# Reading the moving operands of the split products with the words of their two halves in turn

## The chip, the cores and the metric

The kernel runs on one core of one Trainium2 chip. The metric is the device time of one execution, in microseconds, as the median of three runs. The core has five engines that run side by side and wait for one another through semaphores: TensorE (PE, with its weight loads shown as PEld), VectorE (DVE), ScalarE (ACT), GpSimd (POOL, here an issuer of transfers) and SyncE (SP, also an issuer of transfers).

## The reference, cut to what matters

Eight batches of linear attention (8 heads, 576 tokens, 64 wide) feed a gated feed-forward layer over 4608 tokens.

```python
q_s = softmax(q over its last axis);  k_s = softmax(k over the sequence)
kv  = einsum('bhsd,bhse->bhde', k_s, v)
x   = einsum('bhsd,bhde->bhse', q_s, kv)   # -> x: 4608 tokens x 512
gate = sigmoid(x @ w_gate)                 # 512 x 1536
val  = x @ w_val                           # 512 x 1536
out  = (gate * val) @ w_out                # 1536 x 512
```

The three weights come as 64-bit floats and are narrowed on the chip; everything else is in 32-bit floats.

## The kernel before

Tokens go through in nine windows of 512 (`NW`). Window 0 is done while the weights are still being narrowed. For windows 1 to 8 the inner dimension of 1536 is walked in six steps, and one step is `g1` (gate and value for 256 inner columns) followed by `g2` of the step before (the product with `w_out`, added into four accumulators in PSUM). The side work of the next window (softmax of `q` and `k`, the `kv` products, `x` itself in `x_mm`) is laid between them by hand, in `side_a`, `side_b` and `fill`. The order on every engine is the order in which the code is written; nothing reorders it later.

**Split products.** A 32-bit value is written as a high part, which is the value rounded to the type `float32r`, and a low part, the difference. A product is then three matmuls: high times high, high times low, low times high. ScalarE makes the high part (a copy into `float32r`), VectorE the low part (a subtraction). The pairs are `c_hl` (pieces of `x` for `g1`), `wo_hl` and `wo_t` (pieces of `w_out`, the moving operand of `g2`), `x_hl` (window 0's `x`, from inner column block 6 on), and the two `ring` tiles of `qT_split` (the moving operand of `x_mm`). They lie in SBUF as contiguous words, and the matmul reads them as contiguous words. The stationary operands (`a_w`, `s_sb`, `h`, `h_parts`, `kv_sb`) are split too, by other lines.

**Sizes.** One call of `g1` is 7 products of 12 matmuls of 128x128 by 256 columns (L860). One call of `g2` is 25 matmuls (L958): 23 of 512 columns and 2 of 256. There are 48 steps, so 4032 matmuls at L860 and 1200 at L958. In window 0, `g1_0` (L777) and `g2_0` (L826) use plain 32-bit operands for the first blocks, where one matmul becomes two instructions on TensorE, and split operands after that: 144 matmuls at L777 and 84 at L826, of 512 columns. `x_mm` (L659) has 12 products of 512 columns in each window from 1 on, cut in two where a window spans two batches.

**Start.** Until about 26 us there is little for TensorE to do. The kernel fills the gaps with matmuls whose results nobody reads: 11 at first (`warm`, L1179, 32-bit, 128 columns), then two groups between the transposes of `k`. The first group is 4 of 512 `float32r` columns (`warm_whole`, L1194) and 5 in which the 512 columns are one and the same word (`warm_one`, L1198: a step of zero). The second is 5 pairs that use 64 rows each (`warm_rows`, L1187) and 2 more of `warm_whole`. All of them read `kv_sb`, which holds zeros then.

Of the kernel before, what the change touches and what calls it, by code (L numbers as in the profile page):

```python
# [8 lines left out]
F32 = mybir.dt.float32  # L9
# [8 lines left out]
P = 128  # L18
# [3 lines left out]
T = 512  # L22
# [29 lines left out]
def attn_moe(ctx: ExitStack, tc: tile.TileContext, qf, qn, qT, k, kT, v, wg, wv, wo, out):  # L52
# [57 lines left out]
    def flat(ap):  # L110
        return ap.rearrange("p a b -> p (a b)")

# [114 lines left out]
    def wo_hi(j):  # L227
        wo_out[j] = t = whpool.tile([P, 2, DM], F32R, name="wo_hl")
        nc.scalar.copy(out=t[:, 0], in_=wo_t[j // 2][:, j % 2])

    def wo_lo(j):
        t = wo_out[j]
        nc.vector.tensor_tensor(
            out=t[:, 1], in0=wo_t[j // 2][:, j % 2], in1=t[:, 0].bitcast(F32), op=ALU.subtract
        )
# [30 lines left out]
    def wo_split(w, p):  # L266
        for i, t in enumerate(wo_hl[w, p]):
            j = 2 * p + i
            if j in wo_stage:
                x = wo_stage.pop(j)  # L270
                nc.scalar.copy(out=t[:, 0], in_=x)
                nc.vector.tensor_tensor(
                    out=t[:, 1], in0=x, in1=t[:, 0].bitcast(F32), op=ALU.subtract
                )
# [356 lines left out]
    def qT_split(w, hp):  # L631
        t = qT_sb.pop((w, hp))
        hi, lo = (ring.tile([P, T], F32R, name="ring") for _ in range(2))
        nc.scalar.copy(out=hi, in_=t)
        nc.vector.tensor_tensor(out=lo, in0=t, in1=hi.bitcast(F32), op=ALU.subtract)
        qT_hl[w, hp] = (hi, lo)
# [12 lines left out]
    def x_mm(w, hp):  # L649
        qh, ql = qT_hl.pop((w, hp))  # L650
        if w > 1 and hp < 3:
            ps = ps_gv.tile([P, T], F32, name="gv")
        else:
            ps = ps_at.tile([P, T], F32, name="at")
        x_ps[w, hp] = ps
        parts = x_parts(w)
        for lh, rh in ((0, qh), (0, ql), (1, qh)):
            for b, f, t in parts:
                nc.tensor.matmul(  # L659
                    ps[:, f:t], lhsT=kv_sb[:, b % 2, lh, hp], rhs=rh[:, f:t],  # L660
                    start=(lh == 0 and rh is qh and f == 0), stop=(lh == 1 and t == T),
                    skip_group_check=True,
                )
# [30 lines left out]
    def x_split_hi(i):  # L694
        sl = slice(2 * i, 2 * i + 2)
        nc.scalar.copy(out=x_hl[0][:, sl], in_=x_0[:, sl])

    def x_split_lo(i):
        sl = slice(2 * i, 2 * i + 2)
        nc.vector.tensor_tensor(  # L700
            out=x_hl[1][:, sl], in0=x_0[:, sl], in1=x_hl[0][:, sl].bitcast(F32), op=ALU.subtract
        )
# [25 lines left out]
    def c_split_hi(i):  # L728
# [8 lines left out]
        nc.scalar.copy(out=c_hl[i][:, 0], in_=src)  # L737

    def c_split_lo(i):
        hi, lo = (c_hl[i][:, x] for x in range(2))  # L740
        nc.vector.tensor_tensor(
            out=lo, in0=c_src.pop(i), in1=hi.bitcast(F32), op=ALU.subtract
        )
# [16 lines left out]
    def g1_0(j):  # L760
        ps = [ps_gv.tile([P, T], F32, name="gv") for _ in range(2)]
        for n in range(2):
            w = w_f32(j, n)
            for kt in range(NK):
# [3 lines left out]
                else:  # L768
# [5 lines left out]
                    xh, xl = (t[:, kt] for t in x_hl)  # L774
# [41 lines left out]
    def g2_0(j):  # L816
        if j == 0:
            acc_new(0)
        if in_parts(j):
            (h_hi, h_lo), (o_hi, o_lo) = ([t[:, i] for i in range(2)] for t in (h_parts[j], wo_out[j]))  # L820
            pairs = [(h_hi, o_hi), (h_hi, o_lo), (h_lo, o_hi)]
        else:
            pairs = [(h_0[j], wo_t[j // 2][:, j % 2])]
# [26 lines left out]
    def g1(w, p, s_next=None):  # L850
# [4 lines left out]
        def prod(ps, ws, i, first, last):  # L855
            for n in range(2):
                wh, wl = ws(n)
                for kt in range(2):
                    for lh, x in ((wh, 0), (wh, 1), (wl, 0)):
                        nc.tensor.matmul(  # L860
                            ps[:, n], lhsT=lh(kt), rhs=c_hl[i][:, x, kt],
# [78 lines left out]
    def g2(w, at):  # L940
# [6 lines left out]
        for i in range(2):  # L947
            for m in range(NT):
# [7 lines left out]
                for lh, rh, e, halves in order:  # L956
                    es = slice(e * DM // halves, (e + 1) * DM // halves)
                    nc.tensor.matmul(  # L958
                        acc[w][m][:, es], lhsT=h[lh][:, i, sl], rhs=o[i][:, rh, es],
                        start=(at == 0 and i == 0 and lh == 0 and rh == 0),  # L960
                        stop=(at == NS - 1 and i == 1 and lh == 1 and e == halves - 1),
# [177 lines left out]
    many = kv_sb.rearrange("p b i h e -> p (b i h e)")  # L1139
# [41 lines left out]
    beside = ps_at.tile([P, T], F32, name="at")  # L1181

    def warm_rows(n):
        for i in range(n):
            for a, ps in enumerate((idle, beside)):
                sl = slice(a * D, (a + 1) * D)
                nc.tensor.matmul(  # L1187
                    ps, lhsT=many[sl, 0:P], rhs=many[sl, T:2 * T], start=True, stop=True,
                    skip_group_check=True,
                )  # L1190

    def warm_whole(n):
        for i in range(n):
            nc.tensor.matmul(idle, lhsT=many[:, 0:P], rhs=many[:, T:2 * T], start=True, stop=True)  # L1194

    def warm_one(n):
        for i in range(n):
            nc.tensor.matmul(  # L1198
                idle, lhsT=many[:, 0:P], rhs=many[:, T:T + 1].broadcast_to([P, T]),
                start=True, stop=True,  # L1200
            )

# [3 lines left out]
    for i in range(0, NP, 2):  # L1206
# [9 lines left out]
        if i == 0:  # L1216
            warm_whole(4)
            warm_one(5)
        else:
            warm_rows(5)  # L1220
            warm_whole(2)
# [248 lines left out]
```

## Time and profile before

| | us |
|---|---|
| median of three runs | 917.14 (916.32 to 917.47) |
| the profiled execution: its own time | 917.45 |
| the profiled execution: its span on the core | 915.7 |
| TensorE busy (matmuls) in that span | 906.5 |
| VectorE busy | 627.2 |
| ScalarE busy | 496.5 |
| TensorE from the start of the first step of window 1 to the end, on the chain that ended last | 145 to 910 |

The busy time of TensorE counts a matmul until its result is out, while the next one has begun long before; so the time that a matmul costs is read from the distance between starts, and best from a long unbroken run of them. The durations of single matmuls (277 ns for 256 columns) overlap and can't be added.

### The profile page before, as it was taken

The numbers are of one execution on the slowest core, as the hardware profiler recorded it, in microseconds if no ns is written. First come the engines' busy times: TensorE is split into PE (matmuls) and PEld (weight loads), VectorE is DVE, ScalarE is ACT, GpSimd is POOL, SyncE is SP. The second block draws the span as 40 slices with busy tenths as digits, with TensorE's granted clock in tenths as the row PEclk, the third lists the DMA queues.
The fourth block names the chain that finished last, engine by engine and source line by source line (L and its number), as shares of the span: only waits on it lengthen the run. The fifth ranks groups of instructions, "written<-read, shape, count | busy, mean of one in ns | idle before, by whom it ended". The sixth has DMA issues, their size and how long they took to land.

```text
span 915.7 us, 16619 instructions
## 1 busy us (share of the span) xinstructions
PE 906.5 (99%) x6481; PEld 810.1 (88%) x6481; DVE 627.2 (68%) x1021; ACT 496.5 (54%) x845; POOL 186.1 (20%) x342
## 2 busy tenths in 40 slices
PE   8999999999999999999999999999999999999997
PEld 7445788999999999999999999999999999999996
DVE  7899999878686567657684777567755565553332
ACT  6989995657473546363554456445633443443212
POOL 0112112324121222122212121212211222121210
PEclk9999999999999999999999999999999999999999
DMA  9997567987998989997999699969997799668771
GB/s 336 382 357 241 211 237 265 309 314 269 311 331 270 344 248 357 319 276 207 371 318 284 184 360 339 287 196 339 336 271 225 212 276 335 197 194 252 220 206 50
DMA packets 91839, 252.62 MB, mean 276 GB/s; under 512 B 13872, under 2 KB 14128, under 8 KB 91760
## 3 DMA queue, kind: packets, MB, share of 16 engines
q0 software_dynamic: 45200, 163.08, 56.7%
q1 hardware_dynamic: 46560, 88.48, 31.3%
q8 instruction: 51, 0.84, 0.4%
q14 instruction: 28, 0.23, 0.1%
HBM read 217.97 MB, written 33.54 MB: 275 GB/s over the span
## 4 chain that ended last, share of the span: by engine, by line
PE 87%; DVE 5%; DMA 4%; ACT 1%; issue 1%; SPq 1%; ACTq 0%
PE gv L860 48%; PE acc L958 28%; PE gv L777 3%; PE gv L659 2%; PE acc L826 2%; PE at L496 2%; PE at L659 1%; DMA wo_raw<-wo_in 1%; DMA q_b<-q_m_row 1%; DMA lent<-v_in 1%; DMA q_m_row<-q_m 1%; DMA lent<-qf_in 1%; DVE a_w L357 1%; DVE q_m L567 1%; DVE f_w L180 1%
## 5 line engine op out<-in xcount | busy, mean ns | idle before, releaser
L860 PE MATMUL gv<-c_hl,s_sb 128*128 128x256 f32 x2304 | 278.0, 277 | 0.4 <-DMA s_sb<-s 0.4
L860 PEld LDWEIGHTS gv<-c_hl,s_sb 128*128 128x128 f32 x2304 | 269.2, 188 | 0.7 <-DVE x L812 0.6
L860 PE MATMUL gv<-c_hl,a_w 128*128 128x256 f32 x1728 | 221.1, 277 | 0.1
L860 PEld LDWEIGHTS gv<-c_hl,a_w 128*128 128x128 f32 x1728 | 208.5, 188 | 0.5 <-ACT sg L908 0.2
L373 POOL DMA_DIRECT2D s_sb<-s x164 | 88.3, 539 | 281.9 <-PE gv L860 272.2
L958 PE MATMUL acc<-wo_hl,h 128*128 128x512 f32 x589 | 142.6, 391 | 0.0
L958 PE MATMUL acc<-wo_t,h 128*128 128x512 f32 (+1 forms) x613 | 135.8, 372 | 0.0
L958 PEld LDWEIGHTS acc<-wo_t,h 128*128 128x128 f32 x613 | 114.8, 188 | 23.7
L906 DVE TENSOR_TENSOR sg<-gv,sg 128x512 f32<-128x512 f32 x48 | 33.1, 690 | 146.4 <-PE gv L860 146.4
L958 PEld LDWEIGHTS acc<-wo_hl,h 128*128 128x128 f32 x589 | 107.0, 188 | 20.5
L893 ACT COPY sg<-gv 128x512 f32<-128x512 f32 x48 | 28.0, 584 | 110.3 <-PE gv L860 107.7
L908 ACT COPY sg<-gv 128x512 f32<-128x512 f32 x48 | 28.2, 586 | 96.7 <-PE gv L860 96.7
L911 DVE TENSOR_TENSOR sg<-sg 128x512 f32<-128x512 f32 x48 | 33.2, 691 | 52.5 <-ACT sg L908 52.5
L932 DVE TENSOR_TENSOR h<-sg,h 128x1024 fp32r<-128x1024 f32 x48 | 58.8, 1225 | 1.6
L262 POOL DMA_DIRECT2D wo_hl<-wo x44 | 26.1, 592 | 159.8 <-PE acc L958 159.8
L920 DVE TENSOR_TENSOR sg<-sg 128x512 f32<-128x512 f32 x48 | 33.2, 692 | 36.3 <-ACT sg L914 36.3
L914 ACT ACTIVATE sg<-sg 128x512 f32<-128x512 f32 x48 | 30.3, 632 | 46.1 <-DVE sg L913 46.0
L902 ACT COPY sg<-gv 128x512 f32<-128x512 f32 x48 | 28.2, 587 | 36.3 <-PE gv L860 36.3
L899 ACT COPY sg<-gv 128x512 f32<-128x512 f32 x48 | 28.2, 587 | 35.0 <-PE gv L860 35.0
L262 POOL DMA_DIRECT2D wo_t<-wo x45 | 24.2, 539 | 95.8 <-PE acc L958 95.6
L777 PE MATMUL gv<-x,f_w 128*128 128x512 f32 x96 | 42.0, 592 | 0.0
L777 PEld LDWEIGHTS gv<-x,f_w 128*128 128x128 f32 x96 | 18.2, 190 | 23.0 <-issue 21.8
(188 smaller groups left out, 1209.9 us busy)
## 6 DMA issues: line engine op xcount, KB each, us to landing
s_sb<-s POOLq DMA_DIRECT2D x164, 512.0 KB, 6.5
wo_t<-wo POOLq DMA_DIRECT2D x45, 512.0 KB, 6.6
wo_hl<-wo POOLq DMA_DIRECT2D x44, 512.0 KB, 4.4
s<-s_sb POOLq DMA_DIRECT2D x24, 512.0 KB, 7.5
out<-x SPq DMA_DIRECT2D x35, 256.0 KB, 6.8
ring<-k_in SPq DMA_DIRECT2D x28, 256.0 KB, 9.2
ring<-qn_in SPq DMA_DIRECT2D x28, 256.0 KB, 6.3
q_b<-q_m_row SPq DMA_DIRECT2D x56, 128.0 KB, 9.5
```

The lines of the kernel that those rows point to most:

```text
L262: nc.gpsimd.dma_start(out=t.rearrange("p h e -> p (h e)"), in_=wo_dram[j].bitcast(F32R))
L373: nc.gpsimd.dma_start(out=s_of(i).rearrange("p h n e -> p (h n e)"), in_=s_dram[p][:, i * n:(i + 1) * n].bitcast(F32R),)
L777: nc.tensor.matmul(ps[n], lhsT=a, rhs=x, start=(kt == 0 and i == 0), stop=(kt == NK - 1 and i == len(pairs) - 1),)
L860: nc.tensor.matmul(ps[:, n], lhsT=lh(kt), rhs=c_hl[i][:, x, kt], start=(first and n == 0 and kt == 0 and lh is wh and x == 0), stop=(last ...
L899: nc.scalar.copy(out=sg[:, 2], in_=z)
L902: nc.scalar.copy(out=sg[:, 1], in_=y)
L906: nc.vector.tensor_tensor(out=sg[:, 0], in0=rr, in1=sg[:, 0], op=ALU.add)
L911: nc.vector.tensor_tensor(out=sg[:, 3], in0=sg[:, 3], in1=sg[:, 2], op=ALU.add)
L914: nc.scalar.activation(sg[:, 0:2, 0], sg[:, 0:2, 0], AF.Sigmoid)
L920: tt(out=sg[:, 0:2, 0], in0=sg[:, 0:2, 0], in1=sg[:, 0:2, 1], op=ALU.mult)
L932: nc.vector.tensor_tensor(out=lo, in0=sg[:, :, 0], in1=hi.bitcast(F32), op=ALU.subtract)
L958: nc.tensor.matmul(acc[w][m][:, es], lhsT=h[lh][:, i, sl], rhs=o[i][:, rh, es], start=(at == 0 and i == 0 and lh == 0 and rh == 0), stop=( ...
```

## The change

Three helpers are added. `halves` looks at the last axis of a tile as two halves, each contiguous. `apart` looks at a source as pairs of neighbouring words, the even words first and the odd ones after them: it steps two words at a time. `woven` looks at a tile as words of its first half and its second half in turn.

The splits that make moving operands read their source through `apart` and write through `halves`. So the even words land in the first half of the tile and the odd words in the second. The matmuls read the tile through `woven`, and get the words back in their old order: word 0 of half one, word 0 of half two, word 1 of half one, and so on. The two words of a turn lie 512 bytes apart in `c_hl` (256 columns) and 1024 bytes apart in `wo_hl`, `wo_t`, `x_hl` and `ring` (512 columns). What is computed, the order of the columns in PSUM, the tiles, their addresses and all waits stay. The stationary operands and the plain 32-bit products are read as before. In `g2` a variable called `halves` is renamed `parts`.

```diff
+    def woven(x):
+        return x.rearrange("p (two t) -> p t two", two=2)
+
+    def apart(x):
+        if len(x.shape) == 3:
+            return x.rearrange("p k (t two) -> p k two t", two=2)
+        return x.rearrange("p (t two) -> p two t", two=2)
+
+    def halves(x):
+        if len(x.shape) == 3:
+            return x.rearrange("p k (two t) -> p k two t", two=2)
+        return x.rearrange("p (two t) -> p two t", two=2)
...
     def wo_hi(j):
-        nc.scalar.copy(out=t[:, 0], in_=wo_t[j // 2][:, j % 2])
+        nc.scalar.copy(out=halves(t[:, 0]), in_=apart(wo_t[j // 2][:, j % 2]))
...
     def x_mm(w, hp):
-                    ps[:, f:t], lhsT=kv_sb[:, b % 2, lh, hp], rhs=rh[:, f:t],
+                    ps[:, f:t], lhsT=kv_sb[:, b % 2, lh, hp], rhs=woven(rh)[:, f // 2:t // 2],
...
     def c_split_hi(i):
-        nc.scalar.copy(out=c_hl[i][:, 0], in_=src)
+        nc.scalar.copy(out=halves(c_hl[i][:, 0]), in_=apart(src))
     def c_split_lo(i):
         nc.vector.tensor_tensor(
-            out=lo, in0=c_src.pop(i), in1=hi.bitcast(F32), op=ALU.subtract
+            out=halves(lo), in0=apart(c_src.pop(i)), in1=halves(hi.bitcast(F32)),
+            op=ALU.subtract,
         )
...
     def g1_0(j):
-                    xh, xl = (t[:, kt] for t in x_hl)
+                    xh, xl = (woven(t[:, kt]) for t in x_hl)
...
     def g2_0(j):
+            o_hi, o_lo = woven(o_hi), woven(o_lo)
...
     def g1(w, p, s_next=None):
-                            ps[:, n], lhsT=lh(kt), rhs=c_hl[i][:, x, kt],
+                            ps[:, n], lhsT=lh(kt), rhs=woven(c_hl[i][:, x, kt]),
...
     def g2(w, at):
+                    ts = slice(e * HT // parts, (e + 1) * HT // parts)
-                        acc[w][m][:, es], lhsT=h[lh][:, i, sl], rhs=o[i][:, rh, es],
+                        acc[w][m][:, es], lhsT=h[lh][:, i, sl], rhs=woven(o[i][:, rh])[:, ts],
...
-        if i == 0:
-            warm_whole(4)
-            warm_one(5)
-        else:
-            warm_rows(5)
-            warm_whole(2)
+        warm(8)
```

`wo_lo`, `wo_split`, `qT_split`, `x_split_hi` and `x_split_lo` change in the same way as the splits shown. The functions `warm_rows`, `warm_whole` and `warm_one` go, and each of the two groups at the start becomes `warm(8)`: eight 32-bit matmuls of 128 columns on a tile of ones.

On no engine does an instruction of the work change its place. Only the groups of filling matmuls at the start do. On TensorE, from the first transposes of `k` (L466) to the first `kv` products (L482, into the PSUM tiles `at`), the rows before are these, cut where the transposes come again:

```order
L1179 MATMUL gv<-lent 128x128 x11
L466 MATMUL acc<-ident,lent 128x128 x4
L466 MATMUL gv<-ident,lent 64x128
...
L1194 MATMUL gv<-kv_sb 128x512 x4
L1198 MATMUL gv<-kv_sb 128x512 x5
...
L1187 MATMUL gv<-kv_sb 128x512
L1187 MATMUL at<-kv_sb 128x512
...
L1194 MATMUL gv<-kv_sb 128x512 x2
L482 MATMUL at<-lent 128x128 x10
```

With the change, the same place (the lines are numbered anew: `warm` is L1199, the transposes L481, the `kv` products L497):

```order
L1199 MATMUL gv<-lent 128x128 x11
L481 MATMUL acc<-ident,lent 128x128 x4
L481 MATMUL gv<-ident,lent 64x128
...
L1199 MATMUL gv<-lent 128x128 x8
L481 MATMUL acc<-ident,lent 128x128 x4
...
L1199 MATMUL gv<-lent 128x128 x8
L497 MATMUL at<-lent 128x128 x10
```

The transposes and the `kv` products stand where they stood; nine and twelve filling matmuls between them have become eight and eight of another kind.

## Rows read from the trace of the kernel before

**Rows 1.** The page: engines' busy time; the chain that ended last, by line.

```profile
PE 906.5 (99%) x6481; PEld 810.1 (88%) x6481; DVE 627.2 (68%) x1021; ACT 496.5 (54%) x845; POOL 186.1 (20%) x342
...
PE gv L860 48%; PE acc L958 28%; PE gv L777 3%; PE gv L659 2%; PE acc L826 2%; PE at L496 2%; PE at L659 1%; DMA wo_raw<-wo_in 1%; DMA q_b<-q_m_row 1%; DMA lent<-v_in 1%; DMA q_m_row<-q_m 1%; DMA lent<-qf_in 1%; DVE a_w L357 1%; DVE q_m L567 1%; DVE f_w L180 1%
```

**Rows 2.** Stretches: engines' busy us, last the clock, DMA share, GB/s.

```profile
45.00:50.00 5.00, 5.00 (x13) 2.24 (x12) 5.00 (x8) 5.00 (x7) 0.00 (x0) 1.00 1.03 419
300.00:400.00 100.00, 100.00 (x780) 93.65 (x779) 68.97 (x111) 53.09 (x97) 21.37 (x39) 1.00 1.01 310
```

**Rows 3.** Chain, in order of time: start us, us, what and how many.

```profile
91.46 3.06 PE gv L777 x12
...
136.60 5.60 PE gv L777 x24
142.20 2.74 PE acc L826 x12
...
288.81 9.54 PE gv L860 x84
298.34 5.46 PE acc L958 x25
...
318.81 2.31 PE gv L659 x18
321.12 0.77 PE at L659 x6
```

**Rows 4.** TensorE's start, in order of time: start us, us, group, [idle before].

```profile
7.59 1.18 PE L1194 MATMUL gv<-kv_sb 128*128 128x512 f32 x4
8.61 1.25 PE L1198 MATMUL gv<-kv_sb 128*128 128x512 f32 x5
10.55 0.66 PE L466 MATMUL acc<-ident,lent 128*128 128x128 f32 x4 [0.69 <-ACT lent L409]
...
15.69 2.61 PE L482 MATMUL at<-lent 128*128 128x128 f32 x14 [0.69 <-DMA lent<-v_in]
18.23 3.08 PE L482 MATMUL acc<-lent 128*128 128x128 f32 x20
21.24 1.99 PE L621 MATMUL gv<-ident,lent 128*128 128x128 f32 x16
23.06 3.60 PE L683 MATMUL acc<-q,f_last 128*128 128x512 f32 x8
26.50 13.90 PE L777 MATMUL gv<-x,f_w 128*128 128x512 f32 x32
```

**Rows 5.** The same view, from 7.9 to 8.2 us only.

```profile
7.90 0.86 PE L1194 MATMUL gv<-kv_sb 128*128 128x512 f32 x3
```

**Rows 6.** Groups of TensorE by line and shape: busy us, mean ns of one.

```profile
L777 PE MATMUL gv<-x,f_w 128*128 128x512 f32 x96 | 42.0, 592 | 0.0
...
L1198 PE MATMUL gv<-kv_sb 128*128 128x512 f32 x5 | 1.3, 380 | 0.0
```

**Rows 7.** Groups of VectorE: busy us, mean ns of one, idle before.

```profile
L447 DVE TENSOR_TENSOR ring<-ring,kmax_b 128x512 f32<-128x512 f32 x28 | 29.3, 1095 | 0.0
...
L629 DVE TENSOR_TENSOR ring<-ring,q_b 128x512 f32<-128x512 f32 x28 | 17.4, 683 | 0.0
...
L180 DVE SCALAR_TENSOR_TENSOR f_w<-f_w,w_raw 128x512 int32<-128x512 int32 x10 | 6.5, 683 | 0.0
```

**Rows 8.** Groups of ScalarE: the same columns.

```profile
L737 ACT CAST c_hl<-ring 128x512 fp32r<-128x512 f32 x32 | 19.1, 618 | 0.0
...
L173 ACT ACTIVATE f_w<-w_raw 128x512 f32<-128x512 f32 x10 | 6.4, 692 | 0.0
```

**Rows 9.** Who waited for whom: us in total, times, longest us.

```profile
POOL s_sb L373 <- PE gv L860: 272.2, 159, 11.0
POOL wo_hl L262 <- PE acc L958: 159.8, 40, 11.8
DVE sg L906 <- PE gv L860: 146.4, 42, 7.6
```

**Rows 10.** Transfers: KB each, median us from issue to landing.

```profile
s_sb<-s POOLq DMA_DIRECT2D x164, 512.0 KB, 6.5
wo_t<-wo POOLq DMA_DIRECT2D x45, 512.0 KB, 6.6
```

More of the change, by code (lines that the diff above doesn't have):

```diff
@@ L233, in wo_lo @@
         nc.vector.tensor_tensor(
-            out=t[:, 1], in0=wo_t[j // 2][:, j % 2], in1=t[:, 0].bitcast(F32), op=ALU.subtract
+            out=halves(t[:, 1]), in0=apart(wo_t[j // 2][:, j % 2]),
+            in1=halves(t[:, 0].bitcast(F32)), op=ALU.subtract,
         )
@@ L270, in wo_split @@
                 x = wo_stage.pop(j)
-                nc.scalar.copy(out=t[:, 0], in_=x)
+                nc.scalar.copy(out=halves(t[:, 0]), in_=apart(x))
                 nc.vector.tensor_tensor(
-                    out=t[:, 1], in0=x, in1=t[:, 0].bitcast(F32), op=ALU.subtract
+                    out=halves(t[:, 1]), in0=apart(x), in1=halves(t[:, 0].bitcast(F32)),
+                    op=ALU.subtract,
                 )
@@ L633, in qT_split @@
         hi, lo = (ring.tile([P, T], F32R, name="ring") for _ in range(2))
-        nc.scalar.copy(out=hi, in_=t)
-        nc.vector.tensor_tensor(out=lo, in0=t, in1=hi.bitcast(F32), op=ALU.subtract)
+        nc.scalar.copy(out=halves(hi), in_=apart(t))
+        nc.vector.tensor_tensor(
+            out=halves(lo), in0=apart(t), in1=halves(hi.bitcast(F32)), op=ALU.subtract
+        )
         qT_hl[w, hp] = (hi, lo)
@@ L695, in x_split_hi @@
         sl = slice(2 * i, 2 * i + 2)
-        nc.scalar.copy(out=x_hl[0][:, sl], in_=x_0[:, sl])
+        nc.scalar.copy(out=halves(x_hl[0][:, sl]), in_=apart(x_0[:, sl]))
     def x_split_lo(i):
@@ L700, in x_split_lo @@
         nc.vector.tensor_tensor(
-            out=x_hl[1][:, sl], in0=x_0[:, sl], in1=x_hl[0][:, sl].bitcast(F32), op=ALU.subtract
+            out=halves(x_hl[1][:, sl]), in0=apart(x_0[:, sl]),
+            in1=halves(x_hl[0][:, sl].bitcast(F32)), op=ALU.subtract,
         )
@@ L741, in c_split_lo @@
         nc.vector.tensor_tensor(
-            out=lo, in0=c_src.pop(i), in1=hi.bitcast(F32), op=ALU.subtract
+            out=halves(lo), in0=apart(c_src.pop(i)), in1=halves(hi.bitcast(F32)),
+            op=ALU.subtract,
         )
@@ L955, in g2 @@
                         order[2:] = [(1, 0, e, 2) for e in range(2)]
-                for lh, rh, e, halves in order:
-                    es = slice(e * DM // halves, (e + 1) * DM // halves)
+                for lh, rh, e, parts in order:
+                    es = slice(e * DM // parts, (e + 1) * DM // parts)
+                    ts = slice(e * HT // parts, (e + 1) * HT // parts)
                     nc.tensor.matmul(
-                        acc[w][m][:, es], lhsT=h[lh][:, i, sl], rhs=o[i][:, rh, es],
+                        acc[w][m][:, es], lhsT=h[lh][:, i, sl], rhs=woven(o[i][:, rh])[:, ts],
                         start=(at == 0 and i == 0 and lh == 0 and rh == 0),
-                        stop=(at == NS - 1 and i == 1 and lh == 1 and e == halves - 1),
+                        stop=(at == NS - 1 and i == 1 and lh == 1 and e == parts - 1),
                         skip_group_check=True,
@@ L1138, in attn_moe @@
     ones = lent[4][:, NP * S:NP * S + P]
-    many = kv_sb.rearrange("p b i h e -> p (b i h e)")
     k0 = lent[0][:, 0:NP * 4 * P].rearrange("p (h s) -> p h s", s=4 * P)
@@ L1179, in warm @@
             nc.tensor.matmul(idle[:, 0:P], lhsT=ones, rhs=ones, start=True, stop=True)
[L1181 to L1201, printed above, removed]
     warm(11)
```

## The prediction

> **What bounds the kernel now.** I read the page first: TensorE is busy 906.5 us of a span of 915.7, and the chain that ended last lies on its lines, 48% on L860 and 28% on L958 [rows 1]. Next I read the stretches: from 300 to 400 us TensorE has no gap, at a granted clock of 1.00, while VectorE is busy 69 us and ScalarE 53 of 100 [rows 2]. Who waits agrees: VectorE, and GpSimd's transfers, wait for TensorE's products [rows 9]; hardly anything that TensorE waits for is listed. So after the start the time is the number of columns that stream through TensorE, times the time per column. The order of work matters little; what matters is whether a column can be had for less.
>
> That is read from the chain by pieces. A call of L860 is 84 matmuls of 256 columns in 9.54 us, one of L958 is 12,288 columns in 5.46 us [rows 3]. That is 0.4436 ns and 0.4443 ns per column: the same for short and long matmuls, so it is a price of the column and not of the matmul. [...]
> - 4 matmuls at L1194 read 512 different words each. Three of them start at 7.90 us or after and L1198 starts at 8.61 [rows 4, 5]: 0.237 us each.
> - 5 matmuls at L1198 have the same weights, columns and place, but their 512 words are one word read again and again. They take 1.25 us with the last one's tail of 0.38 [rows 4, 6], so (1.25 - 0.38) / 4 = 0.2175 us each: 0.4248 ns per column.
> [...]
>
> So the array itself takes a column in 0.42 ns. [...]
>
> **The change part by part.** *Reading the halves in turn.* [...] No row shows two places read in turn by TensorE, so the price is bounded from both sides. [...] The worst is the last rival below. I take the one-word row, 0.4248, as the nearest: same instruction, same weights beside it, same type.
>
> Per step: 21,504 columns x 0.4248 = 9.13 us for 9.54, and 12,288 x 0.4248 = 5.22 for 5.46: 0.65 us less. Times 48 steps: 31.0 us. In window 0, the split blocks of L777 take 5.60 us for 12,288 columns and of L826 2.74 us for 6,144 [rows 3]; they would take 5.22 and 2.61. With 6 of the first and 7 of the second: 6 x 0.38 + 7 x 0.13 = 3.2 us. `x_mm` (24 matmuls, 2.31 + 0.77 us, for 6,144 columns [rows 3]) costs 0.50 ns per column because it is cut into short pieces; I count no gain there. Sum: 34.2 us off. [...]
>
> *The splits.* ScalarE now reads its source two words apart. L173 does that today: 692 ns for 512, against 618 for the copy that splits `c_hl` in order [rows 8]. The function differs, so 74 ns is an upper bound. There are 56 splits for `c_hl`, 32 for `q`, 12 for `w_out` and 2 of double size for `x`: 104 x 0.074 = 7.7 us of ScalarE's time in the whole run. It hides behind TensorE, as ScalarE has 47 us in 100 free [rows 2]. It isn't hidden in window 0, where ScalarE and VectorE are busy 5.00 of 5 us [rows 2]: there are 9 + 4 splits and two double ones, 1.3 us. I count 0.5 us of that, with 0 and 1.3 as bounds. On VectorE a second input read two words apart is free: L180 takes 683 ns and L629, with both in order, 683 [rows 7]. Its writes stay contiguous within each half. So VectorE: nothing.
>
> *The filling matmuls.* Nine of about 0.23 us become eight 32-bit ones, 16 instructions of some 0.11 to 0.15 us (20 instructions take 3.08 us at L482 [rows 4]): 1.8 to 2.4 us for 2.1. The second group of 1.9 us becomes the same. What follows waits for other engines and for transfers (gaps of 0.69 us twice [rows 4]), so nothing moves: 0. [...]
>
> *What is late next.* A step would last 14.35 us and not 15.00. The loads of `s_sb` take 6.5 us and are issued a whole step ahead; those of `wo` take 6.6 us [rows 10] and have one call of L860, 9.13 us, to land. Both still fit. VectorE's 69 us in 100 become 72.
>
> Sum against the profiled execution: 917.45 - 34.2 + 0.5 = 883.8. The median of the runs before is 0.3 below that execution; I forecast **884**.
>
> **The rivals.**
> *Transfers take a part back.* The DMA engines are busy 1.01 of the time at 310 GB/s [rows 2]. If that were full, a step could not shrink, and 917 would stay. But between 45 and 50 us the same 16 engines moved 419 GB/s at a share of 1.03 [rows 2], so the share counts packets that wait too. What may happen is that `wo`, with some 2.5 us of slack, lands late in some steps: half of the gain lost, about 900.
>
> *The loss is a price of what is fetched, not of the order.* If each run of neighbouring words costs the stream the same gap when it is fetched, whether another is fetched beside it or not, then the same words make the same gaps: 0.444 ns stays. The change then does what it says and nothing follows: 917.5, or up to 918.8 with ScalarE's 1.3 us. For it: the loss is very even, as a fixed price would be. [...]
>
> *The neighbours are thrown away.* If TensorE keeps only the words that it fetched last, the next word is always somewhere else, and every word costs a fetch. It would begin with the first split blocks at about 91 us [rows 3], at every matmul, and it decides as soon as fetching takes longer than one column. VectorE shows such a price: L447 reads one input four words apart and takes 1095 ns for 512, against 683 at L629 [rows 7], so 0.80 ns more per word. On 1.739 million columns that is 1,390 us: 2,310 us. If a word costs what four in order cost now, 4 x 0.444 ns, it is 2,320 us: 3,240 us. For it: L447, and ScalarE's 692 for 618 with only two words apart. Against it: L447 never comes back to a place before 128 other words, while here the next word but one is the neighbour.
>
> [...]
>
> **How the numbers follow.** Less lost in the stream, 884: 0.55. The same, part of it eaten by transfers, 900: 0.10. The loss stays, 917 to 919: 0.15. Neighbours thrown away, 2,310 or more: 0.20. [...] Within the first, the price per column gives 870 (one cycle) to about 895. The range 870 to 925 holds the first three, nearly 8 in 10. What this kernel's measurement can tell from no change is about 0.2%, 1.8 us. Faster by more: 0.65. Slower by more: 0.20 for the last rival and 0.04 for a third one in which ScalarE's cost shows: 0.24. Within: 0.11.
>
> **What would show it.** In the chain of the changed kernel, a call of L860's line should take 9.1 to 9.2 us and one of L958's about 5.2, steadily, at a clock of 1.00; the groups of the `c_hl` splits should stand at up to 692 ns on ScalarE and 684 on VectorE. TensorE should still have no idle time but a few us. If the calls keep 9.54 and 5.46, the loss is a price of the words; if they take several times as long, neighbours are thrown away. If the calls shrink but gaps stand between them, with `wo` or `s_sb` as releaser, the transfers took it back. A gap or slow matmuls before 26 us would be the filling matmuls' doing. The forecast is wrong above all if two places read in turn aren't like one place read slowly.

## The result and the profile after

The changed kernel takes **905.6 us** (905.13 to 907.7, four runs) where the kernel before takes 916.95 (916.32 to 917.47, four runs): a ratio of 0.9881, 95% interval 0.9864 to 0.9898. It is faster, by 11.3 us. The forecast was 884, a gain of 33 us. So the sign was right, and so was the place where the gain was sought, the price of a column: 216 ns for 512 of them where it was 227.5 (5.19 / 24 and 5.46 / 24 us, below). The size was not: two thirds of the expected gain is missing. One execution of experiment 6 was disturbed (938.14 us): it is left out of that run's time, and from its trace only single calls are read. Line numbers have moved: the calls of 84 matmuls are L880 now (`g1`), those of 25 L979 (`g2`), the split blocks of window 0 L796 and L846, `x_mm` L676, the subtraction on `k` (`k_sub`) L462.

The page of the changed kernel: span, busy time by engine, and the chain that ended last, by engine.

```profile
span 904.1 us, 16642 instructions
...
PE 882.4 (98%) x6492; PEld 801.9 (89%) x6492; DVE 648.9 (72%) x1021; ACT 519.1 (57%) x845; POOL 184.3 (20%) x342
...
PE 71%; DVE 10%; ACT 8%; DMA 7%; issue 2%; SPq 1%; POOL 0%; ACTq 0%; DVEq 0%; POOLq 0%
```

TensorE is busy 24 us less than in [rows 1], and the span is only 11.6 shorter. VectorE and ScalarE are busy 22 and 23 us more, with the same number of instructions. Before, TensorE's lines made up 86% of the chain [rows 1]; now they make up 71%. The next two views are the chain by pieces (start us, us, what) and the same stretch as in [rows 2].

```profile
320.90 2.23 PE gv L676 x18
323.13 0.74 PE at L676 x6
323.88 9.38 PE gv L880 x84
333.25 5.19 PE acc L979 x25
```

```profile
300.00:400.00 100.00, 98.13 (x780) 93.26 (x780) 71.93 (x113) 56.02 (x96) 20.98 (x39) 1.00 1.04 312
```

A call of 25 went from 5.46 to 5.19 us (forecast 5.22). A call of 84 went from 9.54 [rows 3] only to 9.38 (forecast 9.13). And TensorE, which had no gap in these 100 us, has 1.87 us of them now. What it waits for (engine and line, releaser: us in total, times, longest us):

```profile
PE gv L880 <- ACT sg L913: 4.4, 7, 0.7
PE acc L846 <- ACT h_parts L812: 2.0, 1, 2.0
...
PE gv L880 <- DVE s_sb L330: 1.4, 2, 0.9
...
PE gv L880 <- DMA s_sb<-s: 1.1, 1, 1.1
PE gv L796 <- DVE ring L650: 1.1, 2, 0.7
PE gv L796 <- ACT v L804: 1.0, 2, 0.8
```

Before, only two waits on these lines were listed, of 0.4 us each. Here is the largest kind, L880 for L913, in the chain of one window.

```profile
269.03 1.23 DVE h L952
270.26 4.00 DVE ring L462 x3
...
274.27 0.63 ACT ring L467
274.90 0.48 ACT sg L913
...
275.43 6.96 PE gv L880 x60
```

L913 is the copy on ScalarE that empties the PSUM tile of the call's first product; the third product needs that tile. On ScalarE the copy stands behind the exponentials of `k` (L467): in ScalarE's timeline the last of them starts at 274.27 us, the copy at 274.81. The exponentials wait for VectorE's subtraction (L462). The subtraction reads `kmax_b` four words apart; no line of it was changed. Its group and those of the splits (busy us, mean ns of one, idle before), with one that reads in order at the end:

```profile
L462 DVE TENSOR_TENSOR ring<-ring,kmax_b 128x512 f32<-128x512 f32 x28 | 36.6, 1357 | 0.0
...
L759 DVE TENSOR_TENSOR c_hl<-ring,c_hl 128x512 fp32r<-128x512 f32 x32 | 24.6, 780 | 0.0
...
L926 DVE TENSOR_TENSOR sg<-gv,sg 128x512 f32<-128x512 f32 x48 | 33.1, 690 | 120.3 <-PE gv L880 120.1 <-issue 0.3
```

```profile
L755 ACT CAST c_hl<-ring 128x512 fp32r<-128x512 f32 x32 | 26.7, 858 | 0.0
```

L462 went from 1095 ns [rows 7] to 1357. The split on ScalarE went from 618 [rows 8] to 858; up to 692 was forecast. The split on VectorE takes 780; 684 was forecast.

**Where the 11.6 us of the two profiled executions lie**, from three starts on TensorE (the first plain 32-bit block of window 0, its first split block, the first call of 84: 26.50, 88.00 and 144.78 before, 27.03, 88.53 and 147.27 after) and the spans' ends. The plain blocks take 61.5 us in both:

| stretch | forecast | measured |
|---|---|---|
| up to the first split block of window 0 | 0 | +0.5 |
| the split blocks, up to the first call of 84 | -2.7 | +2.0 |
| the rest: windows 1 to 8 | -31.0 | -14.1 |
| sum | -33.7 | -11.6 |

In the rest, the 48 calls of 84 add up to 461.4 us before and 461.8 after: what they gained was lost again. Beyond 48 undisturbed calls, of 9.54 and 9.38 us, this is 3.5 us before and 11.6 after; of these 8.1 us more, 6.9 are listed as waits. The calls of 25 (46 of them) went from 252.0 to 239.2, and `x_mm` from 26.1 to 25.3.

### The profile page after: what moved, and what is told of

Same layout as the page of the kernel before. It is cut to its first block, busy times and chain, and to the rows that moved or that the text cites. A ratio compares the mean times of both kernels' runs of the same rounds, so it can differ in the third digit from the quotient of the medians.

```text
span 904.1 us, 16642 instructions
## 1 busy us (share of the span) xinstructions
PE 882.4 (98%) x6492; PEld 801.9 (89%) x6492; DVE 648.9 (72%) x1021; ACT 519.1 (57%) x845; POOL 184.3 (20%) x342
## 4 chain that ended last, share of the span: by engine, by line
PE 71%; DVE 10%; ACT 8%; DMA 7%; issue 2%; SPq 1%; POOL 0%; ACTq 0%; DVEq 0%; POOLq 0%
PE gv L880 41%; PE acc L979 21%; PE gv L796 3%; PE gv L676 1%; DMA q_m_row<-q_m 1%; PE at L511 1%; DMA q_b<-q_m_row 1%; DVE ring L462 1%; DMA s_sb<-s 1%; PE acc L846 1%; DMA s<-s_sb 1%; DMA ring<-qT_in 1%; DMA lent<-v_in 1%; DVE h L952 1%; ACT w_raw L171 1%
## 5 line engine op out<-in xcount | busy, mean ns | idle before, releaser
L880 PE MATMUL gv<-c_hl,s_sb 128*128 128x256 f32 x2304 | 275.8, 276 | 7.0 <-ACT sg L913 4.4
L880 PEld LDWEIGHTS gv<-c_hl,s_sb 128*128 128x128 f32 x2304 | 265.7, 192 | 9.0 <-ACT sg L913 5.8
L880 PE MATMUL gv<-c_hl,a_w 128*128 128x256 f32 x1728 | 217.0, 275 | 0.4 <-DVE c_hl L759 0.4
L880 PEld LDWEIGHTS gv<-c_hl,a_w 128*128 128x128 f32 x1728 | 204.8, 192 | 1.0 <-DVE c_hl L759 0.7
L979 PE MATMUL acc<-wo_hl,h 128*128 128x512 f32 x589 | 135.5, 380 | 0.0
L979 PEld LDWEIGHTS acc<-wo_t,h 128*128 128x128 f32 x613 | 115.5, 189 | 16.3
L979 PE MATMUL acc<-wo_t,h 128*128 128x512 f32 (+1 forms) x613 | 129.7, 362 | 0.0
L979 PEld LDWEIGHTS acc<-wo_hl,h 128*128 128x128 f32 x589 | 107.7, 189 | 13.6
L926 DVE TENSOR_TENSOR sg<-gv,sg 128x512 f32<-128x512 f32 x48 | 33.1, 690 | 120.3 <-PE gv L880 120.1
L913 ACT COPY sg<-gv 128x512 f32<-128x512 f32 x48 | 28.2, 587 | 87.3 <-PE gv L880 84.4
L276 POOL DMA_DIRECT2D wo_hl<-wo x44 | 23.7, 538 | 153.1 <-PE acc L979 153.1
L922 ACT COPY sg<-gv 128x512 f32<-128x512 f32 x48 | 28.3, 590 | 37.3 <-PE gv L880 37.3
L919 ACT COPY sg<-gv 128x512 f32<-128x512 f32 x48 | 28.3, 589 | 30.6 <-PE gv L880 30.6
L462 DVE TENSOR_TENSOR ring<-ring,kmax_b 128x512 f32<-128x512 f32 (+1 forms) x35 | 45.0, 1348 | 0.0
L796 PE MATMUL gv<-x,f_w 128*128 128x512 f32 x96 | 42.0, 592 | 0.0
```

Source lines behind the costliest of these rows:

```text
L276: nc.gpsimd.dma_start(out=t.rearrange("p h e -> p (h e)"), in_=wo_dram[j].bitcast(F32R))
L462: eng.tensor_tensor(out=kt, in0=kt, in1=m, op=ALU.subtract)
L796: nc.tensor.matmul(ps[n], lhsT=a, rhs=x, start=(kt == 0 and i == 0), stop=(kt == NK - 1 and i == len(pairs) - 1),)
L880: nc.tensor.matmul(ps[:, n], lhsT=lh(kt), rhs=woven(c_hl[i][:, x, kt]), start=(first and n == 0 and kt == 0 and lh is wh and x == 0), stop ...
L919: nc.scalar.copy(out=sg[:, 2], in_=z)
L926: nc.vector.tensor_tensor(out=sg[:, 0], in0=rr, in1=sg[:, 0], op=ALU.add)
```

## The experiments

Three questions were open. Why did the call of 84 gain 0.16 us and not 0.41? Where did the waits come from? And what of it can be had back? Times of the kernel before beside these runs were 916.5 to 917.1 us.

**1. What the stream costs, pattern by pattern.** Matmuls are added at the end, in groups of six with one operand pattern each (512 columns, the same weights).

```diff
+    for what in (
+        probe_in_order(),
+        kvf[:, 0:1].broadcast_to([P, T]),
+        wide(256)[:, 0:1].broadcast_to([P, HT, 2]),
+        near(4), near(8), near(16), near(32), near(64), near(128),
+        wide(256), wide(512), wide(1024),
+        kvf[:, 0:T].rearrange("p (four t) -> p t four", four=4),
+        step_by(2), step_by(4),
+        probe_in_order(),
+    ):
+        for _ in range(6):
+            nc.tensor.matmul(seen, lhsT=kvf[:, 0:P], rhs=what, start=True, stop=True)
```

> The changed kernel with 16 groups of 6 matmuls of 512 columns behind its last product, when the other engines have almost nothing left to do. All have the same weights and the same place in PSUM; only the pattern in which the moving words are read differs: in order; one word again and again; two words 1024 bytes apart again and again; words of two neighbouring runs in turn with the two 16, 32, 64, 128, 256, 512, 1024, 2048 and 4096 bytes apart; four quarters in turn; a step of two and of four words; in order again. Distance theory: in order 227 ns from start to start, one word 216, and in turn 216 where the two are 1024 bytes apart or more but about 223 where they are 512 apart. Length theory (the 256-column matmuls miss their price because they are short): 512 bytes gives 216 as well. Kept-lines theory: in turn is as cheap at 16 to 64 bytes as at 1024, since what counts is only that a place has two cycles. A step of four words shows what a place costs that isn't used again: 4 x 227 = 907 by the price of a run of four words, 216 if fetching is never the limit.

The timeline of TensorE at the end, one line for each group (start us, us, group); the nine patterns in turn, from 16 to 4096 bytes apart, stand in one line of 54.

```profile
899.72 1.56 PE L1452 MATMUL gv<-kv_sb 128*128 128x512 f32 x6
...
901.11 1.47 PE L1452 MATMUL gv<-kv_sb 128*128 128x512 f32 x6
...
902.42 1.47 PE L1452 MATMUL gv<-kv_sb 128*128 128x512 f32 x6
...
903.73 11.82 PE L1452 MATMUL gv<-kv_sb 128*128 128x512 f32 x54
...
915.39 1.83 PE L1452 MATMUL gv<-kv_sb 128*128 128x512 f32 x6
...
917.05 2.88 PE L1452 MATMUL gv<-kv_sb 128*128 128x512 f32 x6
...
919.75 2.95 PE L1452 MATMUL gv<-kv_sb 128*128 128x512 f32 x6
...
922.51 1.55 PE L1452 MATMUL gv<-kv_sb 128*128 128x512 f32 x6
```

The price of one is the distance from a group's start to the next one's, over its count. In order: 1.39 / 6 = 232 ns. One word: 1.31 / 6 = 218, and two fixed words the same. In turn: 11.66 / 54 = **216** on the mean of the nine distances; six matmuls at 64 bytes, with the one ahead of them, take 1.67 us, and so do six at 4096. Four quarters in turn: 1.66 / 6 = 277. A step of two words: 2.70 / 6 = 450. A step of four: 2.76 / 6 = 460. So from 16 to 4096 bytes it doesn't matter how far apart two places lie that are read in turn. Why is not shown. With steps a word costs 0.88 to 0.90 ns, and it makes hardly a difference whether one or three neighbours are left out. Neither of the two prices expected for a step of four, 907 and 216 ns, came.

**2. Distance, in the kernel itself.** The two halves of `c_hl` lie 1024 bytes apart and not 512, so that both sizes of matmul read at the same distance.

```diff
-        nc.scalar.copy(out=halves(c_hl[i][:, 0]), in_=apart(src))
+        nc.scalar.copy(out=far_halves(c_hl[i][:, 0]), in_=apart(src))
...
-                            ps[:, n], lhsT=lh(kt), rhs=woven(c_hl[i][:, x, kt]),
+                            ps[:, n], lhsT=lh(kt), rhs=far_woven(c_hl[i][:, x])[:, kt],
```

> The changed kernel with the two words of a turn in c_hl 1024 bytes apart and not 512: a half holds half of the columns of both 128-row blocks. Distance theory: the calls of 84 matmuls fall from 9.38 us to 84 x 0.1095 = 9.2, 48 x 0.18 = 9 us in all, so about 897. Length theory: 9.38 stays and 905.6 with it. If other engines' waits set the pace, the calls fall and the time doesn't.

905.38 us, ratio 0.9884 (0.9855 to 0.9912); the calls of 84 keep 9.38. Distance is not why they gain less.

**3. The weights beside short matmuls.** Again at the end, eight matmuls for each pair of weights and columns, all moving operands in turn.

```diff
+    for weights, columns in (
+        (in_order, T), (in_order, HT), (in_order, 128), (in_order, 64),
+        (by_two, HT), (by_two, 128),
+        (kvf[:, 0:1].broadcast_to([P, P]), HT), (kvf[:, 0:1].broadcast_to([P, P]), 128),
+        (kvf[:, 0:96], HT), (kvf[:, 0:64], HT), (kvf[:, 0:64], 128), (kvf[:, 0:32], 128),
+    ):
```

> The changed kernel with 12 groups of 8 matmuls behind its last product, all with moving words read in turn, 1024 bytes apart. Only the number of moving columns and the stationary operand (every matmul loads it anew) change: 128 columns wide, in order, against 512, 256, 128 and 64 moving columns; 128 wide and read two words apart; 128 wide from one word; 96, 64 and 32 wide. Weight-load theory (a load of 128 columns takes about 111 ns and the next one can start only with the matmul before it, so no matmul with such weights can follow sooner): 512 columns 216, and 256, 128 and 64 columns all 111 to 112; with 64-wide weights 256 columns fall to 109 and 128 columns to 56; with 32-wide ones 128 columns 56. Fixed-cost theory (a short matmul pays more per column by itself): 256 columns 112 whatever the weights are, 128 columns 59 with the wide ones.

The same view (weights' size after the names, then rows x columns):

```profile
897.72 1.89 PE L1438 MATMUL gv<-kv_sb 128*128 128x512 f32 x8
...
899.45 1.05 PE L1438 MATMUL gv<-kv_sb 128*128 128x256 f32 x8
...
900.34 1.00 PE L1438 MATMUL gv<-kv_sb 128*128 128x128 f32 x8
...
901.18 1.03 PE L1438 MATMUL gv<-kv_sb 128*128 128x64 f32 x8
...
906.67 1.04 PE L1438 MATMUL gv<-kv_sb 128*64 128x256 f32 x8
...
907.54 0.63 PE L1438 MATMUL gv<-kv_sb 128*64 128x128 f32 x8
```

With weights 128 wide, 512 columns take 216 ns and 256 take 0.89 / 8 = 111; but 128 columns still take 0.84 / 8 = 105, and 64 take 0.86 / 8 = 107 (the next group starts at 902.04). With weights 64 wide, 256 columns take 0.87 / 8 = 109, and 128 take 58 from start to start (0.63 us less the tail of 0.22, over 7). So in a run of matmuls that each load new weights of 128 columns, one takes 105 to **112 ns** even with a half or a quarter of the 256 columns: a floor. The calls of 84 are made of just such matmuls, of 256 columns: 84 x 0.1117 = 9.38 us.

**4. The filling matmuls alone.** The kernel before, with `warm(8)` twice at the start.

```diff
-            warm_whole(4)
-            warm_one(5)
...
-            warm_rows(5)
-            warm_whole(2)
+        warm(8)
```

> The kernel before with the filling matmuls of the changed one and nothing else. By the prediction nothing moves: 917. The trace of the changed kernel shows the first product with w_gate 0.53 us later (27.03 for 26.50 us); if the filling matmuls do that, this kernel shows it too, and 917.5.

917.03 us, ratio 0.9998 (0.9985 to 1.0012). The medians show no cost of theirs.

**5. Splits that read in order, matmuls that read in turn.** The columns of the split products then come out in another order than they should.

```diff
     def apart(x):
-        return x.rearrange("p (t two) -> p two t", two=2)
+        return x.rearrange("p (two t) -> p two t", two=2)
```

> The changed kernel, but the splits read their source in order and not two words apart. The moving words then come in another order than the columns are meant to have; the reading of them is as in the changed kernel. If the step of two words is what makes the splits slow (ScalarE 616 to 860 ns, VectorE 684 to 775), they are back at 616 and 684, and window 0 gets back the 2 us that it lost between 88 and 147 us: 902 to 903. If the splits are slow because TensorE's reading in turn crowds everyone, they stay slow and the time stays at 905.6. The three-word-apart subtraction of k (1095 to 1357 ns) isn't touched; if the waits of 1 us a window come from it, they stay.

903.61 us, ratio 0.9851 (0.9837 to 0.9866).

```profile
L462 DVE TENSOR_TENSOR ring<-ring,kmax_b 128x512 f32<-128x512 f32 x28 | 36.5, 1350 | 0.0
...
L759 DVE TENSOR_TENSOR c_hl<-ring,c_hl 128x512 fp32r<-128x512 f32 x32 | 21.3, 684 | 0.0
```

The splits are back at 684 (ScalarE: 615), and the kernel gains 2 us, no more. The split blocks of window 0, which were to get 2 us back, still take 58.7 us up to the first call of 84. The subtraction on `k` stays slow and the five calls before the `k` products still take 10.5 us. So what the splits cost is hidden but for some 2 us; and what slows L462 is not the splits beside it. TensorE's reading is left, and experiment 7 tells it apart call by call.

**6. The row that L462 reads four words apart, sent in the order in which it is read**, in the changed kernel and in the one before. That transfer then moves 512 single words.

```diff
-out=row.rearrange("(p h) -> p h", h=NP), in_=kmax.pop(b))
+out=row.rearrange("(h p) -> p h", h=NP), in_=kmax.pop(b))
...
-        m = m.rearrange("s (p h) -> s h p", h=NP)
```

> The changed kernel with the maxima of k sent to memory in the order in which the subtraction reads them, so that it reads both inputs in order and no longer one of them four words apart. Wait theory (the subtraction, 1357 ns now and 1095 before, holds back the last exponential on ScalarE and with it the copy that frees a PSUM tile for TensorE, 0.85 to 1.0 us in each window from 3 on): it falls to 684, the calls of 84 before the k products fall from 10.5 to 9.38 us, six windows x 1.1 = 6.6 us off 905.6: about 899, and a little less than that where windows 1 and 2 gain too. Rival (something else is late right behind it, or the transfer of single words is slow and comes late): 903 to 906.

> The kernel before with the maxima of k sent in reading order and nothing else. The subtraction should fall from 1095 to 684 ns. Wait theory: TensorE hardly waits for it here, since the copy that frees the PSUM tile was done some 0.5 us ahead, so the time stays at 917. If it gained as much as it does in the changed kernel, the subtraction would be a cost of its own and not one that the reading in turn brought.

925.48 us, ratio 1.0098 (1.0057 to 1.0139), and 928.27, ratio 1.0130 (1.0113 to 1.0146): both slower, a miss. The cure has a price of its own. The transfer, in the table of transfers of the changed kernel and of this run (KB each, median us to landing):

```profile
kmax_row<-k_max SPq DMA_DIRECT2D x5, 2.0 KB, 4.4
```

```profile
kmax_row<-k_max SPq DMA_DIRECT2D x5, 2.0 KB, 9.9
```

It lands 5.5 us later and holds up what stands behind it. On GpSimd's queue, which sends two of the rows, it lands after 11.2 us for 3.8 (in the kernel before, 11.4 for 4.1), and there the first split block of window 0 begins 7.8 us later than before (95.81 for 88.00): most of what that variant loses. In the changed kernel's variant L462 is at 687 ns, and the call before the `k` products takes 9.5 us in three of five windows, not 10.5. Two steps on, a call takes some 17 us in three windows; there a load of `k` (`kt<-kT_in`), which SyncE issues behind the row, comes last. This bears out the cause, but it is no remedy.

**7. In turn for `w_out` alone.** `c_hl`, `x_hl` and the `q` tiles are in order again.

```diff
-                            ps[:, n], lhsT=lh(kt), rhs=woven(c_hl[i][:, x, kt]),
+                            ps[:, n], lhsT=lh(kt), rhs=c_hl[i][:, x, kt],
```

> The changed kernel with only the product with w_out reading in turn; c_hl, x_hl and the tiles of q are split and read in order as before. Calls of 25 should take 5.19 us as in the changed kernel, calls of 84 9.54 as before: 48 x 0.27 = 13 us off 917 if no wait comes: 904. The splits of c_hl and q should be back at 616 and 684 ns. If reading in turn by itself slows the four-words-apart subtraction, it stays above 1095, but less than 1357, since only a third of TensorE's time reads in turn; if the waits before the k products go with it, the two changes weigh the same and this is within 2 us of the full change's 905.6.

912.32 us, ratio 0.9947 (0.9931 to 0.9964): 904 was expected, a miss. Two neighbouring pieces of its chain late in the run, and L462:

```profile
809.61 9.89 PE gv L877 x84
819.50 5.18 PE acc L976 x25
```

```profile
L462 DVE TENSOR_TENSOR ring<-ring,kmax_b 128x512 f32<-128x512 f32 x28 | 31.9, 1199 | 0.0
```

The calls of 25 keep their whole gain. The calls of 84, in order again, don't go back to 9.54 alone: eleven take 9.89 or 9.90 without a wait, 117 to 118 ns for a matmul, among them all of the last window. Why they vary is open.

The 1199 ns of L462 are a mean of two kinds. One of each (start us, us): the first lies wholly beneath a call of 84, which reads in order here, the second wholly beneath a call of 25, which reads in turn.

```profile
260.64 1.09 DVE L462 TENSOR_TENSOR ring<-ring,kmax_b 128x512 f32<-128x512 f32 x1
...
269.58 1.54 DVE L462 TENSOR_TENSOR ring<-ring,kmax_b 128x512 f32<-128x512 f32 x1
```

All five that lie wholly beneath a call of 25 take 1.54 us; all that lie wholly beneath a call of 84 take 1.07 to 1.11. In the kernel before it is 1.09 beneath calls of 25 and 1.07 to 1.11 beneath calls of 84, and in the changed kernel, where both read in turn, 1.53 to 1.55 beneath calls of 25 and 1.31 to 1.39 beneath calls of 84. So within one execution the subtraction is slow just while TensorE reads in turn. Whether the pattern does it or the pace of TensorE, which is 5% quicker with it, no run separates.

**8. The last exponential of `k` behind the copy.** In the side work for windows 3 to 7, the one of 64 rows is written after the copy that empties the PSUM tile, not ahead of it. Everything else is the changed kernel.

```diff
-                    for t in range(5):
+                    for t in range(4):
                         k_exp(b, t)
+                    fill[0] = [lambda: k_exp(b, 4)]
```

> The changed kernel with one instruction of ScalarE moved in windows 3 to 7: the last exponential of k (64 rows) stands behind the copy that frees the PSUM tile for the next call of L860's line, and no longer ahead of it. Wait theory: the five calls of 84 before the k products fall from 10.5 us to 9.4, and 905.6 to about 900.5. If TensorE's 1 us there comes from something else (a transfer, the slower splits), nothing changes: 905.6.

**900.19 us**, ratio 0.9816 (0.9801 to 0.9830). ScalarE at the place of the chain above (start us, us, instruction):

```profile
272.82 0.65 ACT L467 ACTIVATE ring<-ring 128x512 f32<-128x512 f32 x1 [0.49 <-DVE ring L462]
273.37 0.56 ACT L913 COPY sg<-gv 128x512 f32<-128x512 f32 x1
274.05 0.63 ACT L467 ACTIVATE ring<-ring 64x512 f32<-64x512 f32 x1
```

The copy starts 1.7 us after the call (271.65), where it was 3.0 in the changed kernel; the third product no longer waits. The five calls of 10.5 us take 9.5. L462 itself is as slow as it was (1346 ns); it only doesn't matter.

**9. Two more ways to make the splits cheaper.** The step of two words moved from the `c_hl` splits into the copies out of PSUM; the `q` tiles in order; and both of these with experiment 8.

```diff
+            out=x_32[:, hp].rearrange("p (th two t) -> p th two t", th=2, two=2),
+            in_=x_ps.pop((w, hp)).rearrange("p (th t two) -> p th two t", th=2, two=2),
...
-        nc.scalar.copy(out=halves(c_hl[i][:, 0]), in_=apart(src))
+        nc.scalar.copy(out=c_hl[i][:, 0], in_=src)
```

```diff
-                    ps[:, f:t], lhsT=kv_sb[:, b % 2, lh, hp], rhs=woven(rh)[:, f // 2:t // 2],
+                    ps[:, f:t], lhsT=kv_sb[:, b % 2, lh, hp], rhs=rh[:, f:t],
```

> The changed kernel, with the step of two words moved from the splits of c_hl to the copy that brings x out of PSUM: four copies a window read PSUM two words apart and write x in the order even words, odd words; the four differences and the 14 splits behind them read SBUF in order. The splits should be back at 616 (ScalarE) and 684 ns (VectorE) from 860 and 775. By the run with the splits' source in order the gain is 1 to 2 us (903.6 there); if a copy out of PSUM pays for the step (590 to some 860), it is still four instead of 14. Rival: the splits hide behind TensorE in every window from 2 on, and the time stays within 1 us of 905.6.

> The changed kernel with the tiles of q split and read in order as before. The products of x lose 0.1 us a window (25.3 to 26.1 us in all); the 32 splits of q fall from 847 to 616 ns and from 793 to 684. If the late pieces of window 0 (from 88 to 147 us it takes 58.7 us where it took 56.8) come from these splits, it gains 1 to 2 us; if from others, it is 0.8 us slower.

> The three together: the exponential behind the copy, the step of two words in the copies out of PSUM, q in order. If each takes away a wait of its own, the sum is about 905.6 - 5 - 2 - 0.5 = 898; if they share one, 900.

904.92 us (ratio 0.9871, 0.9856 to 0.9886), 905.77 (0.9877, 0.9861 to 0.9894) and 900.05 (0.9815, 0.9800 to 0.9829). With the first, the splits are back at 616 and 685 ns while the copies out of PSUM stay at 587, yet the time moves within its uncertainty; the third equals experiment 8. The splits of windows 1 to 8 are hidden, as the prediction said.

**10. Window 0's `x` in order**, in the changed kernel and together with experiment 8.

```diff
-                    xh, xl = (woven(t[:, kt]) for t in x_hl)
+                    xh, xl = (t[:, kt] for t in x_hl)
```

> The changed kernel with only x_hl (the moving operand of window 0's split products with w_gate and w_val) split and read in order as before. Those calls of 24 go back from 5.2 to 5.6 us when nothing holds them up, 2.3 us more in all. If the narrowing of the weights (reads two words apart, 683 to 850 ns and 690 to 998 ns between 88 and 147 us) is slow because TensorE reads in turn, it comes back to 683 to 750 there, and window 0's stretch from the first split block to the first step of window 1, 58.7 us in the changed kernel and 56.8 before, falls to about 57: 904. If the stretch is paced by something else, it grows by up to 2.3 us: 906 to 908.

> The kernel with the exponential behind the copy (900.2) and x_hl in order. If window 0 gets its 1 to 2 us back: 898.5 to 899. If not: 900 to 902.

903.16 us (ratio 0.9854, 0.9840 to 0.9869), and **898.52** (0.9814, 0.9795 to 0.9832), the fastest median of all. Groups of VectorE and of ScalarE that narrow the last weights, from 88 to 147 us: first the changed kernel, then the same with window 0's `x` in order.

```profile
L193 DVE SCALAR_TENSOR_TENSOR f_last<-f_last,w_raw 128x512 int32<-128x512 int32 x4 | 3.2, 838 | 0.0
L164 DVE TENSOR_SCALAR w_raw<-w_raw 128x1024 uint32<-128x1024 uint32 x2 | 1.8, 924 | 0.0
...
L186 ACT ACTIVATE wo_t<-wo_raw 128x512 f32<-128x512 f32 x6 | 5.1, 856 | 0.0
```

```profile
L193 DVE SCALAR_TENSOR_TENSOR f_last<-f_last,w_raw 128x512 int32<-128x512 int32 x4 | 2.6, 684 | 0.0
...
L164 DVE TENSOR_SCALAR w_raw<-w_raw 128x1024 uint32<-128x1024 uint32 x2 | 1.4, 704 | 0.0
...
L186 ACT ACTIVATE wo_t<-wo_raw 128x512 f32<-128x512 f32 x6 | 4.5, 742 | 0.0
```

The narrowing reads every second word. Nothing of it is edited here; only `x_hl` is, its splits and TensorE's reading of it. The groups shown take 13 to 24% less, close to the 683, 690 and 714 ns of the kernel before. Others gain little (`wo_t` on VectorE, 794 to 760 ns) or nothing (`f_w<-w_raw` on ScalarE, 850 to 848), and the products with `w_out` still read in turn beside them. From the first split block to the first call of 84 the kernel now takes 57.3 us, against 58.7; the wait of 2.0 us on `h_parts` is 0.6. In window 0, where the other engines are the bound, TensorE's faster reading costs more than it brings: 2.4 us by the medians against the changed kernel. The 1.7 us against experiment 8 lie within the spread (897.82 to 901.67, and 899.59 to 900.97).

## Why the prediction was right and wrong

**What bounds the kernel, and that its columns can be had for less: right.** Two places read in turn give 216 ns for 512 columns, steadily, where the calls of 25 had 227.5 [rows 3]. Why columns in order take longer is not shown. The price that I took from the one-word row, 0.4248 ns or 217.5 ns for 512, was good to 1%. For the calls of 25 the forecast of 5.22 us met 5.19. In window 0 the two blocks of 24 without a wait inside, the last two, take 5.18 us, and a block of 12 takes 2.59, a little less than forecast. No run shows the one cycle per column from which the range's lower end, 870, was worked out; the runs showed no less than these 216 ns for 512, 0.422 ns for one column.

**The price of a call of 84: wrong, 12 us.** The step that failed is "the same for short and long matmuls, so it is a price of the column and not of the matmul". That 256 columns cost half of 512 was read from the kernel before, where 113.5 ns lay just above a second limit. At 112 ns (9.38 us / 84) the weight load takes over (experiment 3). The gain of a call is 0.16 us and not 0.41: 48 x 0.25 = 12.0 us short. The view had a sign of it that I showed and didn't use: weight loads were busy 93.65 of 100 us [rows 2]. In the probe 256 columns take 111 ns with weights 128 wide and 109 with weights 64 wide, and 128 columns take 105 and 58. The forecast's 108.75 ns for 256 columns are reached with weights 64 wide and not with weights 128 wide.

**"VectorE: nothing" and 74 ns on ScalarE: wrong in size, and it missed the instruction that counts.** The prices were taken from rows where TensorE read in order or plain 32-bit operands. While it reads in turn, instructions of VectorE and ScalarE that step over words in SBUF get slower (L462 by 262 ns; ScalarE's split by 240 and not 74), and those that read in order don't (L926: 690, as before). Experiments 5, 7 and 10 show that this comes with TensorE's reading in turn. The splits hide nearly all of it. L462, which the diff doesn't touch and the prediction only used as a price, doesn't.

**"What is late next": the question was right, the answer incomplete.** I looked at transfers and at the sum of VectorE's time and not at the one copy on which a product waits. The call and its copy in the kernel before, and the copy in the changed one (start us, us):

```profile
270.95 9.54 PE gv L860 x84
```

```profile
272.50 0.56 ACT L893 COPY sg<-gv 128x512 f32<-128x512 f32 x1
```

```profile
274.81 0.56 ACT L913 COPY sg<-gv 128x512 f32<-128x512 f32 x1
```

Before, the copy started 1.55 us after its call began. Now it starts 2.96 us after (its call begins at 271.85). Of these 1.41 us, 0.97 are three slower subtractions (3.10 us before, 4.07 now) and 0.43 the shorter pair of calls ahead of it (9.54 + 5.46 against 9.38 + 5.19). The third product wants the tile 2.7 us after the call's start, so before the copy was in time and now it isn't. Five such waits cost 5 of the 8.1 us that the calls of 84 lost again; experiment 8 gives them back. The rest is spread over windows 1 and 2: 1.4 us on L330, and 1.1 on one late transfer, which is all that came of the rival "transfers take a part back".

**Window 0: wrong, 4.7 us.** The sum gave each block the gain of one that nothing holds up, and such a block gains a little more than that (5.60 to 5.18, 2.74 to 2.59). But four of the six blocks of 24 wait inside, and the six went only from 35.1 to 34.3 us together, where 2.3 had been forecast. The six of 12 in this stretch went from 16.5 to 15.6. Against that stand 2.2 us behind the fifth block of 24 (the wait on `h_parts`) and 1.4 more between the other blocks (5.2 to 6.6): 2.0 us longer in all. The bounds of 0 to 1.3 us counted the splits' longer reads and not the slower narrowing, in a stretch where [rows 2] show both engines full. Experiment 10 brings 1.4 us of it back by the profiles and some 2 by the medians. The rest stays open: from run to run of the kernels that read `x_hl` in turn the stretch varies from 58.5 to 60.5 us.

**The filling matmuls: right.** Nothing within 0.15% (experiment 4). The 0.5 us up to the split blocks are no more than scatter: in the traces with the new filling the first plain block begins between 26.1 and 28.3 us.

**The other rivals.** A price of what is fetched fell: the same words cost 232 ns in order and 216 in turn. The neighbours are not thrown away either: with the next word in another place each time, up to 4096 bytes away, 512 columns take 216 ns, the least of all patterns. A price for words left out is real, 450 ns at a step of two and 460 at a step of four, not the four times that the prediction gave as one bound.

The sum, then: 12.0 us from the weight loads' floor, 8.1 that the calls of 84 lost again, mostly in waits, 4.7 in window 0, 0.5 at the start, less some 3 that the calls of 25 and the pieces between calls did better: 22 us, which is 33.7 - 11.6. That 905.6 lies between 870 and 925 is luck: the range was that wide for rivals that didn't come true, not for these terms.

## What to carry to other kernels

A price per column that holds for two lengths shows that no other limit binds at this price; before a cheaper one is put in, look for the limit right beneath it, here the weight loads at 94% busy. An access pattern of the bounding engine can slow others, as it took L462 from 1095 to 1357 ns; so ask which of their instructions step over words, and which copy in front of the bounding engine has the least slack, even if the diff touches neither. Where a stage is bound by those others, leave the pattern out (window 0's `x` in order: 903.16 us for 905.6); and a copy that frees a tile goes ahead of work that can wait (experiment 8: 900.19).

## What the runs showed of the hardware that was not expected

- While TensorE reads in turn, stepped reads of VectorE and ScalarE are slower: 1.09 to 1.54 us at four words apart beneath a call of 25 (experiment 7), and 714 to 856 ns at two words apart on ScalarE (the narrowing of `wo_t` in window 0, kernel before and changed one); L926, which reads in order, stays at 690. Why isn't shown.
- Reading in order has more than one pace: for 512 columns 237 ns at L1194 [rows 4, 5], 232 in the first group of experiment 1 and 227.5 in the calls of 25 of the kernel before, and for 256 columns 113.5 or 117 to 118 ns in experiment 7. Reading in turn gave 216 for 512 each time (5.19 / 24, 11.66 / 54 and 1.73 / 8 us).
- In a run of matmuls with new weights of 128 columns each, one takes 111 ns with 256 moving columns, 105 with 128 and 107 with 64 (experiment 3); with weights of 64 columns 256 take 109 and 128 take 58.
- A transfer of 2 KB in single words landed after 9.9 us, where runs of four words took 4.4.
